# Where the low halves of the expert weights are made: VectorE in place of GpSimd

## The chip, the cores and the metric

The program runs on one core of a Trainium2 chip. The metric is the device time of one execution in microseconds. Five engines work on it, each through its own queue in order: TensorE (PE in the profile, its weight loads PEld), VectorE (DVE), ScalarE (ACT), GpSimd (POOL), and SyncE (SP), which here only issues transfers.

## The reference

A small attention in two resolutions makes a matrix `x` of 4608 tokens by 512; the tokens are then dealt out to 8 experts, 576 to each, and each expert is a two-layer network. The part that matters here, cut to its core:

```python
def _moe_ref(x, w_gate, w1, w2):            # w1: (8, 512, 1024), w2: (8, 1024, 512)
    N, D = x.shape
    E = w_gate.shape[1]
    cap = N // E
    order = np.argsort(-(x @ w_gate).flatten())
    ...                                     # best (token, expert) pairs first, until an expert is full
    for e in range(E):
        mask = assigned == e
        h = np.maximum(x[mask] @ w1[e], 0.0)
        out[mask] = h @ w2[e]
```

## The kernel before, in words

The first part (class `Attention`, up to about 294 us) makes `x`, writes it to memory and keeps the logits of all tokens. The second part has two strands that run into each other.

*Routing* (class `Routing`, lines 626 to 995) finds the tokens of one expert after another, and each list depends on the one before. `setup` prepares keys. `count` narrows a threshold in three steps, twice for each expert: VectorE compares the keys with a row of thresholds (`cmp`, line 702); TensorE counts them (line 728); VectorE brings the counts back (`cs`, line 734); TensorE adds them up (line 737); VectorE compares with the capacity (`fl`, line 740); TensorE spreads the answer (line 742); VectorE takes the maximum (`nj`, line 744) and makes the next thresholds (`thr`, `rest`, lines 748 and 751), the last time the value (`val`, line 755). Then the number of the expert is known (`ei`, line 853), which starts the loads of its weights. `emit` turns the chosen tokens into the list `idx`: VectorE makes one-hot rows (`ohh`, `r`, `ohl`, lines 970 to 982), TensorE multiplies them (line 985), and line 994 writes the list.

*Experts* (class `Experts`). `weights` loads the raw weights into `nat`, four pieces of 128 x 2048 for each expert out of a pool of six. `gather` fetches the tokens' rows with GpSimd's indirect transfers (`xg`, line 1062), makes a high half on ScalarE and a low half on VectorE (`xs`, lines 1081 and 1082), and has SP transpose them (`xt`, line 1083). `mlp` multiplies in fp16 with halves: 192 matmuls `pH` (line 1098) for the hidden layer, with `ht` made by ScalarE and VectorE after each of eight groups (lines 1111 and 1114), then 120 matmuls `pX` (line 1127) for the output `y` (line 1132), which GpSimd scatters to memory (line 1135).

`split` makes the halves of the weights, in eight pieces `k` of 128 x 1024. `wh` is the high half and `wl` the low one, the scaled weight less `wh`. For the first four pieces of the first expert (`FV`) ScalarE writes `wh` straight from the raw weights and VectorE makes `wl` in one instruction. For the 60 others ScalarE first scales the raw weights in place (line 1045), then casts them to `wh` (line 1046), and GpSimd subtracts in four pieces of `LOP` = 256 columns (line 1048).

When `split` runs is set in the loop over the experts: the pieces of expert i + 1 are asked for behind `ht` of group f of expert i (`in1`), or, while the first expert runs, behind the outputs `y` (`in2`). The order on each engine comes from a scheduler with priorities: routing has the higher priority, and other work is put where the scheduler expects an engine to be free. The order is fixed when the program is built.

Of the kernel before, what the change touches and what calls it, by code (L numbers as in the profile page):

```python
# [11 lines left out]
AF = mybir.ActivationFunctionType  # L12
OP = mybir.AluOpType
# [605 lines left out]

W1S, W2S, XM = 64.0, 64.0, 8.0  # L620
LOP = 256
CAP = NTOK // E
LV = ((64, 1024), (32, 32), (32, 1))
SW = 16
HALF = {16: ((0, NT),), 32: ((0, 20), (20, NT)), 64: ((0, 20), (20, NT)), 128: ((0, 12), (12, 24), (24, NT))}
LOV = ()
FV = (0, 1, 2, 3)
XSB = 2
LOE = "vector"
RACT = True  # L630
# [367 lines left out]
class Experts:  # L998
# [32 lines left out]
    def split(self, raw, first):  # L1031

        nc = self.nc
        w = {}

        def piece(k):
            r = raw[k // 2][:, 1024 * (k % 2):1024 * (k % 2) + 1024]
            hi = self.wt.tile([128, 1024], F16, name=f"wh{k}")
            lo = self.wt.tile([128, 1024], F16, name=f"wl{k}")
            sc = W1S if k < 4 else W2S  # L1040
            if first and k in FV or k in LOV:
                nc.scalar.activation(hi, r, AF.Copy, scale=sc)
                nc.vector.scalar_tensor_tensor(lo, r, sc, hi, op0=OP.mult, op1=OP.subtract)
            else:
                nc.scalar.activation(r, r, AF.Copy, scale=sc)  # L1045
                nc.scalar.copy(hi, r)  # L1046
                for a in range(0, 1024, LOP):
                    nc.gpsimd.tensor_tensor(lo[:, a:a + LOP], r[:, a:a + LOP], hi[:, a:a + LOP], op=OP.subtract)  # L1048
            w[k] = (hi, lo)

        return w, piece
# [217 lines left out]
```

## Time and profile before

| what | us |
|---|---|
| three runs | 824.54, 828.63, 828.93 (median 828.63) |
| the profiled execution | 830.1 |
| its span in the trace | 828.3 |
| TensorE busy | 691.8 |
| VectorE busy | 531.8 |
| ScalarE busy | 394.0 |
| GpSimd busy | 401.7 |
| mean granted clock of TensorE | 0.923 |

An engine's busy time is the union of its instructions. A row of a group reads: line, engine, operation, output and inputs by the program's names, shapes, how many; then the busy time and the mean of one in ns; then the idle time of the engine just before them and what ended it. A row of stretches has the stretch in us from the span's start, its length, then busy time and number of instructions for each engine, the granted clock, the share of the transfer engines and GB/s. A row of the timeline has start, duration, engine, line and what it does; in the chain of waits, start, duration, engine and line.

The first matmul of an expert starts at 332.6 us. The first list is written at 322.3 us, the last at 620.4.

### The profile page before, as it was taken

Reading aid. Unit: us, or ns where it says so; the run is one execution under the profiler, and the core shown is the slowest. Engines: PE = TensorE matmul, PEld = TensorE weight load, DVE = VectorE, ACT = ScalarE, POOL = GpSimd, SP = SyncE. Lnnn points to the kernel's source line nnn. Section 1 sums busy time; section 2 is a strip of 40 time slices with the busy share of each in tenths; the row PEclk is TensorE's granted clock in tenths of the full one; section 3 lists DMA queues with packets and bytes.
Section 4 is the critical chain, followed back from the end, with each engine's and each line's share of the span. In section 5 each row is a group of like instructions: output and inputs, shape, how many; then the busy total and the mean of one; then the engine's idle time right before and its main releaser. Section 6 shows DMA issues by size and latency. Waiting matters only on the chain.

```text
span 828.3 us, 21421 instructions
## 1 busy us (share of the span) xinstructions
PE 691.8 (84%) x8545; PEld 473.2 (57%) x8545; DVE 531.8 (64%) x1555; ACT 394.0 (48%) x691; POOL 401.7 (48%) x514
## 2 busy tenths in 40 slices
PE   6688979887898832997888967798989999999995
PEld 4577868776786731653364445445536657474752
DVE  6878888986879878787795758969682222122210
ACT  3356757565485412535564225425625638284210
POOL 8355373562635403417758335436544838474001
PEclk9689999998999965999897999999999999999998
DMA  9949979899897614317352570565184563703101
GB/s 256 204 141 227 275 191 274 214 220 259 193 262 193 188 40 132 130 66 215 90 210 58 124 252 9 196 154 172 53 194 82 205 169 102 160 13 87 29 15 44
DMA packets 152904, 126.19 MB, mean 152 GB/s; under 512 B 96997, under 2 KB 127205, under 8 KB 152805
## 3 DMA queue, kind: packets, MB, share of 16 engines
q1 hardware_dynamic: 145424, 103.30, 48.7%
q0 software_dynamic: 6432, 20.98, 8.2%
q8 instruction: 68, 1.11, 0.6%
q10 hardware_dynamic: 948, 0.55, 0.2%
q14 instruction: 32, 0.25, 0.1%
HBM read 95.30 MB, written 21.23 MB: 141 GB/s over the span
## 4 chain that ended last, share of the span: by engine, by line
PE 37%; DVE 27%; DMA 14%; issue 11%; ACT 4%; SPq 3%; POOL 2%; another core or an unknown queue 1%; ACTq 0%; POOLq 0%; DVEq 0%
PE pH L1098 14%; PE pX L1127 8%; DVE cmp L702 4%; DMA xt<-xs 3%; PE pR L728 2%; DMA nat<-in_v_dram 2%; PE g L476 2%; DVE ht L1114 2%; PE g L436 1%; DMA vw<-in_v_dram 1%; PE g L292 1%; SPq L200 1%; DMA up_dram<-xu 1%; DMA nat<-in_q_dram 1%; PE g L373 1%
## 5 line engine op out<-in xcount | busy, mean ns | idle before, releaser
L1098 PE MATMUL pH<-xt,wh 128*128 128x256 f16 (+1 forms) x1024 | 203.8, 294 | 1.8 <-DMA xt<-xs 0.8
L1048 POOL TENSOR_TENSOR wl<-nat,wh 128x256 f16<-128x256 f32 x240 | 163.1, 712 | 77.1 <-issue 45.1
L1127 PE MATMUL pX<-wh,ht 128*128 128x512 f16 (+1 forms) x640 | 185.6, 386 | 0.0
L1098 PE MATMUL pH<-xt,wl 128*128 128x320 f16 (+1 forms) x512 | 150.0, 293 | 0.0
L1127 PEld LDWEIGHTS <-ht 128*128 128x128 f16 (+1 forms) x960 | 82.1, 101 | 88.2 <-issue 6.7
L1127 PE MATMUL pX<-wl,ht 128*128 128x512 f16 (+1 forms) x320 | 120.0, 386 | 0.0
L1098 PEld LDWEIGHTS <-wh 128*128 128x128 f16 x1024 | 99.8, 100 | 32.5 <-issue 7.0
L1135 POOL DMA_INDIRECT out_dram<-y,idx x40 | 44.9, 1121 | 135.6 <-ACT y L1132 115.7
L1114 DVE SCALAR_TENSOR_TENSOR ht<-pH,ht 128x512 f16<-128x512 f32 (+1 forms) x128 | 52.4, 450 | 70.7 <-ACT ht L1111 70.5
L1111 ACT ACTIVATE ht<-pH 128x512 f16<-128x512 f32 (+1 forms) x128 | 45.5, 407 | 97.1 <-PE pH L1098 97.1
L1132 ACT ACTIVATE y<-pX 128x512 f32<-128x512 f32 (+1 forms) x40 | 23.8, 594 | 132.5 <-PE pX L1127 107.4
L1062 POOL DMA_INDIRECT xg<-x_dram,idx x40 | 42.4, 1059 | 64.4 <-DMA nat<-in_moe_w_dram 32.3
L1046 ACT CAST wh<-nat 128x1024 f16<-128x1024 f32 x60 | 62.5, 1044 | 1.5
L1045 ACT ACTIVATE nat<-nat 128x1024 f32<-128x1024 f32 x60 | 62.8, 1058 | 0.0
L465 ACT COPY pt<-g 64x512 f32<-64x512 f32 x72 | 41.8, 581 | 37.4 <-PE g L454 36.3
L1098 PEld LDWEIGHTS <-wl 128*128 128x128 f16 x512 | 51.1, 100 | 12.8
L1082 DVE SCALAR_TENSOR_TENSOR xs<-xg,xs 128x512 f16<-128x512 f32 (+1 forms) x35 | 23.9, 701 | 53.6 <-ACT xs L1081 46.4
L292 PE MATMUL g<-ident,nat 128*128 128x128 f32 x256 | 41.0, 287 | 15.3 <-DMA nat<-in_q_dram 11.7
L265 POOL TENSOR_TENSOR gtmp<-kt 128x576 f32<-128x576 f32 x7 | 8.3, 1186 | 85.9 <-ACT kt L278 50.6
L476 PE MATMUL g<-vw,pt 128*64 128x65 f32 x1152 | 46.8, 236 | 2.6 <-DMA up_dram<-xu 1.4
L265 POOL TENSOR_TENSOR gtmp<-qz 64x576 f32<-64x576 f32 x28 | 32.4, 1157 | 29.5 <-DVE kdt L268 27.8
L476 PEld LDWEIGHTS g<-vw,pt 128*64 128x64 f32 x1152 | 41.6, 149 | 8.9 <-ACT pt L465 5.1
(222 smaller groups left out, 1282.4 us busy)
## 6 DMA issues: line engine op xcount, KB each, us to landing
nat<-in_moe_w_dram SPq DMA_DIRECT2D x28, 1024.0 KB
vw<-in_v_dram SPq DMA_DIRECT2D x136, 96.0 KB
up<-up_dram SPq DMA_DIRECT2D x36, 256.0 KB
x_dram<-x SPq DMA_DIRECT2D x36, 256.0 KB
nat<-in_q_dram SPq DMA_DIRECT2D x16, 512.0 KB
nat<-in_k_dram SPq DMA_DIRECT2D x16, 512.0 KB
nat<-in_v_dram SPq DMA_DIRECT2D x14, 512.0 KB
up_dram<-xu SPq DMA_DIRECT2D x16, 128.0 KB
```

Source lines behind the costliest of these rows:

```text
L292: nc.tensor.transpose(p[:, a, :, fp], src[:, 4 * hh + 2 * a + s, 2 * fp:2 * fp + 2].rearrange("p f d -> p (f d)"), self.ident)
L465: self.nc.scalar.copy(out, in_)
L476: nc.tensor.matmul(o[64 * i:64 * i + 64, 65 * h:65 * h + 65], pt[:, 2 * g + i, h].rearrange("p b q -> p (b q)"), self.vw[u % 4][:, i, 4 * ...
L1045: nc.scalar.activation(r, r, AF.Copy, scale=sc)
L1046: nc.scalar.copy(hi, r)
L1048: nc.gpsimd.tensor_tensor(lo[:, a:a + LOP], r[:, a:a + LOP], hi[:, a:a + LOP], op=OP.subtract)
L1062: self.fetched = nc.gpsimd.indirect_dma_start(out=xg[:n], out_offset=None, in_=self.x, in_offset=bass.IndirectOffsetOnAxis(ap=idx[:n, c:c ...
L1098: mm = nc.tensor.matmul(p[:, s, :s1 - s0], w[d][a][:, 128 * f:128 * f + 128], xt[:, b, d, s0:s1], start=j == 0, stop=j == len(seq) - 1)
L1111: last = nc.scalar.activation(hi, q, AF.Relu)
L1114: nc.vector.scalar_tensor_tensor(lo, q, 0.0, hi, op0=OP.max, op1=OP.subtract)
L1127: nc.tensor.matmul(p[o:o + m], ht[:, f, h0:h0 + m], w[4 + f // 2][b][:, 512 * (f % 2):512 * (f % 2) + 512], start=j < parts, stop=j >= len ...
L1135: i = nc.gpsimd.indirect_dma_start(out=self.out, in_=y[:n], in_offset=None, out_offset=bass.IndirectOffsetOnAxis(ap=idx[:n, c:c + 1], axis=0))
```

## The change

Every piece of every expert is now made as the first four were: ScalarE writes `wh` from the raw weights in one pass with the scale, and VectorE makes `wl` from the raw weights and `wh`, but in two instructions of 512 columns instead of one of 1024. There is no scaling pass any more, the raw weights are not written, and GpSimd has only its indirect transfers, the loads of the first expert's second layer and what it does in the attention.

```diff
-LOP = 256
+LOP = 512
-LOV = ()
-FV = (0, 1, 2, 3)
...
-            if first and k in FV or k in LOV:
-                nc.scalar.activation(hi, r, AF.Copy, scale=sc)
-                nc.vector.scalar_tensor_tensor(lo, r, sc, hi, op0=OP.mult, op1=OP.subtract)
-            else:
-                nc.scalar.activation(r, r, AF.Copy, scale=sc)
-                nc.scalar.copy(hi, r)
-                for a in range(0, 1024, LOP):
-                    nc.gpsimd.tensor_tensor(lo[:, a:a + LOP], r[:, a:a + LOP], hi[:, a:a + LOP], op=OP.subtract)
+            nc.scalar.activation(hi, r, AF.Copy, scale=sc)
+            for a in range(0, 1024, LOP):
+                nc.vector.scalar_tensor_tensor(lo[:, a:a + LOP], r[:, a:a + LOP], sc, hi[:, a:a + LOP],
+                                               op0=OP.mult, op1=OP.subtract)
```

The scheduler orders the second part anew. In the changed kernel lines from 627 on are two to six lower than in the profile of before (`cs` 734 is 732, `fl` 740 is 738, `wl` 1048 is 1041).

VectorE, just behind the list `idx` of the second expert, where the count for the third begins. Before:

```order
L734 TENSOR_SCALAR cs<-pR 128x16
L994 TENSOR_TENSOR idx<-sm 32x5
L994 TENSOR_TENSOR idx<-sm 32x4 x2
L740 TENSOR_TENSOR fl<-pR,cap 64x8
L744 TENSOR_REDUCE nj<-pR 128x1
L748 SCALAR_TENSOR_TENSOR thr_6802<-nj,tabs 128x32
L751 SCALAR_TENSOR_TENSOR rest<-nj,tabs 128x33
L702 TENSOR_TENSOR cmp_6806<-xh,thr_6802 128x640
L702 TENSOR_TENSOR cmp_6806<-xh,thr_6802 128x512
```

The same steps now:

```order
L732 TENSOR_SCALAR cs<-pR 128x16
L1041 SCALAR_TENSOR_TENSOR wl_6546<-nat,wh_6545 128x512
L738 TENSOR_TENSOR fl<-pR,cap 64x8
L1041 SCALAR_TENSOR_TENSOR wl_6587<-nat,wh_6586 128x512
L742 TENSOR_REDUCE nj<-pR 128x1
L1041 SCALAR_TENSOR_TENSOR wl_6587<-nat,wh_6586 128x512
L746 SCALAR_TENSOR_TENSOR thr_6770<-nj,tabs 128x32
L749 SCALAR_TENSOR_TENSOR rest<-nj,tabs 128x33
L1041 SCALAR_TENSOR_TENSOR wl_6592<-nat,wh_6591 128x512
L700 TENSOR_TENSOR cmp_6774<-xh,thr_6770 128x640
L700 TENSOR_TENSOR cmp_6774<-xh,thr_6770 128x512
```

Four pieces of 512 columns of the low halves of the second expert's weights now stand between the steps of the count that finds the third expert. It goes on so, on VectorE in the changed kernel:

```order
L1076 SCALAR_TENSOR_TENSOR xs<-xg,xs 128x512 x2
L732 TENSOR_SCALAR cs<-pR 128x32
L1041 SCALAR_TENSOR_TENSOR wl_6592<-nat,wh_6591 128x512
L738 TENSOR_TENSOR fl<-pR,cap 32x8
L1041 SCALAR_TENSOR_TENSOR wl_6629<-nat,wh_6628 128x512
L742 TENSOR_REDUCE nj<-pR 128x1
```

In the next step, too, a piece now stands ahead of `fl` and of `nj`, where the kernel before had none.

TensorE at the same place, between the sums of the counts (line 737) and the spreading of the answer (line 742). Before:

```order
L737 MATMUL pR<-cs,id_5478 32x8
L1127 LDWEIGHTS ht
L1127 MATMUL pX<-wh_6277,ht 128x512
L1127 LDWEIGHTS ht
L1127 MATMUL pX<-wh_6277,ht 128x512
L742 LDWEIGHTS one
L742 MATMUL pR<-fl,one 128x8
```

Now:

```order
L735 MATMUL pR<-cs,id_5478 32x8
L1121 LDWEIGHTS ht
L1121 MATMUL pX<-wh_6383,ht 128x512
L1121 LDWEIGHTS ht
L1121 MATMUL pX<-wl_6384,ht 128x512
L1121 LDWEIGHTS ht
L1121 MATMUL pX<-wh_6383,ht 128x512
L740 LDWEIGHTS one
L740 MATMUL pR<-fl,one 128x8
```

TensorE has three matmuls of the experts there instead of two; over the whole routed part it has 960 `pH` and 502 `pX` up to the last list, where it had 768 and 434.

GpSimd, from the second expert's gathers on. Before:

```order
L1062 DMA xg<-x_dram,idx 128x512 x4
L1062 DMA xg<-x_dram,idx 64x512
L1135 DMA out_dram<-y,idx 4608x512
L1048 TENSOR_TENSOR wl_6601<-nat,wh_6600 128x256 x4
L1048 TENSOR_TENSOR wl_6609<-nat,wh_6608 128x256 x4
L1135 DMA out_dram<-y,idx 4608x512
L1048 TENSOR_TENSOR wl_6649<-nat,wh_6648 128x256 x4
L1048 TENSOR_TENSOR wl_6657<-nat,wh_6656 128x256 x4
L1135 DMA out_dram<-y,idx 4608x512
```

Now:

```order
L1056 DMA xg<-x_dram,idx 128x512 x4
L1056 DMA xg<-x_dram,idx 64x512
L1129 DMA out_dram<-y,idx 4608x512 x3
L1056 DMA xg<-x_dram,idx 128x512 x4
L1056 DMA xg<-x_dram,idx 64x512
```

Only gathers and scatters are left in its queue.

## The prediction

> **What bounds the kernel now.** I read the page's engine totals, then its slices of time.
>
> ```profile
> PE 691.8 (84%) x8545; PEld 473.2 (57%) x8545; DVE 531.8 (64%) x1555; ACT 394.0 (48%) x691; POOL 401.7 (48%) x514
> PE   6688979887898832997888967798989999999995
> DVE  6878888986879878787795758969682222122210
> ```
>
> The experts fill the last 24 slices. In the first fourteen of them VectorE stands at 5 to 9 and TensorE at 6 to 9; in the last ten VectorE has almost nothing to do and TensorE is full. The border is the end of routing, so I cut there with the view by stretches: the second, fourth, fifth, sixth and seventh list of tokens (each stretch from one `idx` to the next), the whole routed stretch, and the rest.
>
> ```profile
> core 0: us, PE busy (x) PEld busy (x) DVE busy (x) ACT busy (x) POOL busy (x), PEclk, DMA share, GB/s
> 383.10:436.00 52.90, 43.97 (x321) 24.16 (x320) 42.06 (x121) 29.30 (x44) 35.40 (x45) 0.87 0.51 142
> 483.00:537.00 54.00, 39.78 (x362) 25.91 (x358) 40.24 (x124) 23.34 (x37) 28.74 (x38) 0.94 0.38 137
> 537.00:576.30 39.30, 34.86 (x289) 18.65 (x289) 31.46 (x115) 14.74 (x26) 19.24 (x18) 1.00 0.55 146
> 576.30:611.90 35.60, 32.44 (x288) 18.81 (x285) 27.87 (x111) 16.43 (x25) 19.25 (x27) 1.00 0.37 118
> 611.90:620.50 8.60, 6.60 (x41) 3.14 (x40) 5.97 (x19) 1.76 (x3) 3.47 (x3) 0.89 1.20 210
> 332.60:620.50 287.90, 243.36 (x1961) 138.96 (x1961) 222.55 (x743) 123.76 (x200) 150.15 (x187) 0.94 0.47 137
> 620.50:818.40 197.90, 196.87 (x1295) 120.91 (x1293) 39.94 (x85) 92.26 (x151) 93.53 (x129) 1.00 0.36 94
> ```
>
> After 620.5 TensorE idles 1.0 us: that part only loses if something becomes late. Before it, TensorE idles 287.9 - 243.4 = 44.5 us; the second and fourth lists cost 8.9 and 14.2 of it, the fifth and sixth 4.4 and 3.2. The same stretches for the experts' own matmuls (line 1098, then line 1127), and the chain of waits for two full halves of an expert:
>
> ```profile
> 332.60:620.50 287.90, 118.33 (x768) 71.45 (x767) 0.94 0.47 137
> 332.60:620.50 287.90, 103.98 (x434) 35.91 (x435) 0.94 0.47 137
> 628.95 23.62 PE pH L1098 x192
> 652.58 23.43 PE pX L1127 x120
> ```
>
> At 0.123 and 0.195 us each they need 768 x 0.123 + 434 x 0.195 = 179.2 us of the 287.9. Routing and transposes take 243.4 - 179.2 = 64.2, idling 44.5. Who waits there, from the view of waits (engine line, releaser, us in total, times, longest):
>
> ```profile
> POOL wl L1048 <- ACT wh L1046: 23.3, 6, 9.7
> PEld L728 <- DVE cmp L702: 17.5, 24, 2.3
> DVE nj L744 <- PE pR L742: 16.2, 33, 0.9
> DVE fl L740 <- PE pR L737: 12.1, 25, 1.3
> PE pR L728 <- DVE cmp L702: 9.3, 14, 2.0
> DVE cs L734 <- PE pR L728: 8.6, 20, 1.6
> PE pR L985 <- DVE ohl L982: 7.6, 5, 5.3
> ```
>
> TensorE waits for VectorE's comparisons and one-hot rows (`cmp`, `ohl`); VectorE waits back in short gaps of about half a microsecond (`nj`, `fl`, `cs`, 36.9 us). So the bound there is a chain going back and forth between the two, with TensorE's matmuls in a fixed order around it.
>
> **Why VectorE is slow there.** Two pairs of rows of VectorE's timeline, and GpSimd's beside the second:
>
> ```profile
> 360.39 0.83 DVE L702 TENSOR_TENSOR cmp<-xl,thr 128x640 bf16<-128x640 int16 x2
> 405.90 3.38 DVE L702 TENSOR_TENSOR cmp<-xl,thr 128x640 bf16<-128x640 int16 x2
> 363.37 0.16 DVE L755 TENSOR_TENSOR val<-nj,rest 128x1 f32<-128x1 f32 x1
> 394.77 1.33 DVE L755 TENSOR_TENSOR val<-nj,rest 128x1 f32<-128x1 f32 x1
> 319.18 0.75 DVE L982 TENSOR_TENSOR ohl<-pl,io 128x576 bf16<-128x576 int16 x1
> 406.44 2.55 POOL L1048 TENSOR_TENSOR wl<-nat,wh 128x256 f16<-128x256 f32 x4
> ```
>
> The same pair of instructions takes 0.83 us alone and 3.38 while GpSimd subtracts; one element costs 1.33 instead of 0.16. Groups by shape from 332 to 620 us:
>
> ```profile
> L982 DVE TENSOR_TENSOR ohl<-pl,io 128x576 bf16<-128x576 int16 x14 | 13.2, 952 | 0.0
> L702 DVE TENSOR_TENSOR cmp<-xl,thr 128x512 bf16<-128x512 int16 x12 | 8.0, 669 | 0.0
> L755 DVE TENSOR_TENSOR val<-nj,rest 128x1 f32<-128x1 f32 x12 | 3.9, 325 | 0.4
> ```
>
> Taking off their calm durations (0.75, 0.42 and 0.16 us) leaves 2.8 + 3.0 + 2.0 = 7.8 us; the same subtraction over all the shapes of that view gives about 37 us. So VectorE's 222.6 us hold between 7.8 and 37 of collision with GpSimd; I take 37, since the excess sits almost wholly in instructions that overlap a subtraction. With 7.8 alone VectorE's need below would be 277 us instead of 248, 3 us short of TensorE's. [...]
>
> **The change part by part.**
>
> ```profile
> L1048 POOL TENSOR_TENSOR wl<-nat,wh 128x256 f16<-128x256 f32 x240 | 163.1, 712 | 77.1 <-issue 45.1 <-ACT wh L1046 23.3 <-POOL wl L1048 8.5
> L1045 ACT ACTIVATE nat<-nat 128x1024 f32<-128x1024 f32 x60 | 62.8, 1058 | 0.0
> L1062 POOL DMA_INDIRECT xg<-x_dram,idx x40 | 42.4, 1059 | 64.4 <-DMA nat<-in_moe_w_dram 32.3 <-DVE xs L1082 18.4 <-issue 5.5
> L1082 DVE SCALAR_TENSOR_TENSOR xs<-xg,xs 128x512 f16<-128x512 f32 (+1 forms) x35 | 23.9, 701 | 53.6 <-ACT xs L1081 46.4 <-DMA xg<-x_dram,idx 6.4 <-issue 0.7
> 326.24 1.22 DVE L1043 SCALAR_TENSOR_TENSOR wl<-nat,wh 128x1024 f16<-128x1024 f32 x1
> ```
>
> Removed: 240 subtractions on GpSimd (163.1 us), and 60 scalings on ScalarE (62.8 us). GpSimd's own time is free; what counts is the collision. ScalarE is 43% busy in the routed stretch (123.8 of 287.9), so its saving is hidden, except that a low half can begin 1.06 us earlier. GpSimd keeps its gathers and scatters of about 1.1 us, no longer queued behind subtractions; that is hidden by the matmuls between `idx` and the next expert.
>
> Added: 128 pieces of 512 columns less the four whole ones. Price of one: no row shows it, but `xs` is the same operation on the same types and size, 0.70 us; half of the whole piece (1.22) is 0.61. Between neighbours the ends overlap, so I take 0.62. The first eight stand ahead of 332 us, 0.16 us more per whole piece, covered by the wait for the gathered rows. By the order of the new program 88 of the 128 stand in the routed part, 32 after it beside full matmuls (20 us on an engine that has 158 us free).
>
> Moved: the routed part now ends later in the experts' work. By the order TensorE has 960 `pH` and 502 `pX` matmuls of the experts up to the last list, not 768 and 434: 118.1 + 98.0 = 216.1 us, with 576 and 458 left (160.3). So TensorE needs 216.1 + 64.2 = 280.3 us in it. VectorE needs 222.6 - 37 + 88 x 0.62 + 8 (eight more pairs of `ht` at about 0.8, three `xs`) = 248. In the order a piece now stands ahead of nearly every `fl`, `nj` and `thr` of the second list, that is in the 0.5 us gaps; each delays the chain by some 0.2 us, while TensorE got more matmuls there.
>
> What TensorE then idles: at least 0; at most what VectorE's whole old idling (287.9 - 222.6 = 65.3) would cause, 248 + 65.3 - 280.3 = 33. I take the rate of the calmest list, 3.2 us for each of six plus 2.0 for the last (short) one, 21.2, since GpSimd no longer collides. Gain 44.5 - 21.2 = 23.3.
>
> New waits: `wl` now waits in VectorE's queue for `wh` of ScalarE and the weights' loads, with routing behind it. How far ahead the loads are, from the timelines of VectorE and SP (the expert's number, the loads, the one-hot rows):
>
> ```profile
> 366.76 0.14 DVE L853 TENSOR_SCALAR ei<-code 1x1 int32<-1x1 f32 x1
> 367.70 2.43 SPq L1025 DMA_DIRECT2D nat<-in_moe_w_dram  x4
> 377.36 2.36 DVE L982 TENSOR_TENSOR ohl<-pl,io 128x576 bf16<-128x576 int16 x2
> ```
>
> The loads are issued 1 to 3.4 us after the number; by the order the first `wl` stands behind the `ohl` rows, 13 us after it. So I cost this 0 and price the other case below. On SP the first two loads of the last expert now stand ahead of the transposes for the sixth; they wait for `wl` pieces that end before those transposes are ready: 0. At the border of the first two experts ScalarE's last `xs` now stands behind the last `y`, and VectorE, SP and TensorE's first `pH` over the later columns wait for it: 0 to 4 us, I take 1.5.
>
> Clock: TensorE's granted clock is 0.94 in the routed stretch and 1.00 after it, 0.87 where it idles much: about 0.06 x 288 = 17 us at most. With half the idling I take 4, between 0 and 17. [...] TensorE's longest wait in the list of 0.87:
>
> ```profile
> PE pR L728 <- DVE cmp L702: 3.3, 3, 2.0
> ```
>
> [...]
>
> **Sum** against the profiled execution (830.1 us, of which the span is 828.3): 828.3 - 23.3 + 1.5 - 4 = 802.5, 25.8 less. The median of the three runs is 828.6, so the forecast is 803 us.
>
> **Rivals.** 1. VectorE full: its short gaps are not filled but added to, all 65.3 us of idling stay. TensorE then idles 33 us: 828.6 - 11.5 + 1.5 = 819 us. For it: 248 of 280 us is 88% busy; against it: pieces stand in the very gaps.
> 2. Slower: GpSimd's waits for `wh` (23.3 us, one of 9.7) come over to VectorE's queue, with `fl`, `nj` and `cmp` behind them, on top of rival 1. TensorE idles 33 + 23.3 = 56.3: 828.6 + 11.8 + 1.5 = 842 us. It decides from VectorE idling some 75 us in the routed part. For it: a queue in order; against it: those waits came from ScalarE standing behind matmuls, and GpSimd was ahead of its time.
> 3. Nothing: the collision is off the path and the chain is bound by round trips; then the new pieces cost what the collision did, 828 us. Against it: in us, idling goes with GpSimd's work (8.9 and 14.2 beside 35.4 and 28.7, but 4.4 and 3.2 beside 19.2 and 19.3). For it: as a share of its stretch GpSimd is as busy in the sixth list (54%) as in the fourth (53%).
>
> **Numbers.** Forecast (788 to 814) 0.61, rival 1 0.16, rival 2 0.14, rival 3 0.09. Within 0.5% is 4 us, about what a measurement can tell here. Faster takes the forecast and rival 1, 0.77; same 0.09; slower 0.14. The range leaves out rival 2 and a little below: low 787 is an idling of 10 us and 8 us of clock (828.6 - 34.5 - 8 + 1.5), high 829.
>
> **What would show it.** No subtraction on GpSimd; `cmp` of 512 columns at 0.42 us throughout, `val` at 0.16; `wl` at 0.6 to 0.7 us; the last `idx` near 632, not 620 (332.6 + 280.3 + 21.2 + 1.5 - 4), but 160 us of full matmuls behind it, not 198; TensorE idling about 21 us ahead of it; the clock above 0.94. The forecast is wrong if VectorE's waits for `wh` or for SP's loads reach 20 us, or TensorE's waits for `fl` and `cs` grow to what `cmp` lost.

## The result, and the profile after

The changed kernel takes 802.43 us in the median of four runs (797.46 to 807.51). Beside it the kernel before took 828.78. The ratio is 0.968, interval 0.9624 to 0.9737. The profiled execution is one of the two short ones: 797.6 us with a span of 795.8.

The totals of the engines and their slices of time, from the page after:

```profile
PE 682.5 (86%) x8545; PEld 470.8 (59%) x8545; DVE 561.6 (71%) x1679; ACT 333.2 (42%) x631; POOL 236.9 (30%) x274
PE   6687979797898853599789799999899979999994
DVE  6878887887788877788769689888869235172210
```

GpSimd loses 165 us, ScalarE 61, VectorE gains 30. The stretches that answer to those of before follow, in the same columns: the second, fourth, fifth, sixth and seventh list, the whole routed part, and what stands behind it.

```profile
382.10:434.80 52.70, 45.42 (x385) 28.07 (x382) 41.66 (x143) 22.33 (x40) 9.19 (x8) 0.94 0.50 150
484.90:526.20 41.30, 40.70 (x327) 21.97 (x323) 37.31 (x131) 12.76 (x24) 11.25 (x10) 1.00 0.55 157
526.20:572.80 46.60, 44.08 (x385) 26.92 (x385) 40.95 (x145) 18.76 (x35) 8.24 (x7) 1.00 0.45 140
572.80:611.20 38.40, 37.94 (x347) 24.26 (x344) 30.23 (x123) 13.40 (x24) 7.98 (x8) 1.00 0.68 197
611.20:621.40 10.20, 9.87 (x62) 4.83 (x60) 9.97 (x27) 3.29 (x6) 1.77 (x2) 1.00 0.53 151
330.70:621.40 290.70, 272.40 (x2238) 161.44 (x2238) 242.76 (x851) 105.14 (x194) 54.37 (x49) 0.97 0.51 153
621.40:786.00 164.60, 158.11 (x1018) 95.51 (x1016) 51.35 (x97) 50.34 (x96) 26.53 (x28) 0.99 0.35 83
```

The routed part is as long as before (290.7 us against 287.9), but TensorE does more in it: of the experts' own matmuls 960 `pH` and 520 `pX`, against 768 and 434. It idles 18.3 us instead of 44.5. What is left behind it is 164.6 us and not 197.9. There a new idle time of some 6 us has come in, where 1.0 was. The fourth list, which had lost 14.2 us of TensorE's time, loses 0.6 now.

VectorE's short instructions from 332 to 620 us by shape, and the pieces of the low halves in the whole program:

```profile
L980 DVE TENSOR_TENSOR ohl<-pl,io 128x576 bf16<-128x576 int16 x14 | 10.2, 750 | 0.0
L700 DVE TENSOR_TENSOR cmp<-xl,thr 128x512 bf16<-128x512 int16 x12 | 5.0, 417 | 0.0
L753 DVE TENSOR_TENSOR val<-nj,rest 128x1 f32<-128x1 f32 x12 | 1.9, 155 | 0.2
L1041 DVE SCALAR_TENSOR_TENSOR wl<-nat,wh 128x512 f16<-128x512 f32 x128 | 85.2, 683 | 2.6 <-ACT wh L1039 0.2
```

All three are at their calm durations, 0.75, 0.42 and 0.16 us, where their means had been 0.95, 0.67 and 0.33. The last row also answers rival 2: ahead of 128 pieces VectorE waited 2.6 us in all. The view of waits for the routed part:

```profile
DVE nj L742 <- PE pR L740: 11.7, 21, 0.9
ACT xs L1075 <- DMA xt<-xs: 10.7, 8, 2.5
DVE cs L732 <- PE pR L726: 6.7, 13, 1.6
DVE fl L738 <- PE pR L735: 6.6, 15, 0.6
PEld L726 <- DVE cmp L700: 5.9, 15, 1.2
```

TensorE's weight loads had waited 17.5 us for `cmp`; now it is 5.9. VectorE's own gaps ahead of `nj`, `fl` and `cs` shrank from 36.9 to 25.0 us, since pieces stand in them. The second row is a wait that has grown, from 4.5 us before: ScalarE's `xs` waits until a transpose has read the old rows and the buffer is free.

The new idle time behind the last list, in the view of TensorE's waits from 621.4 us on; then the timelines of SP and of ScalarE:

```profile
PE pH L1092 <- DMA xt<-xs: 4.9, 2, 4.7
```

```profile
612.98 6.81 SPq L1023 DMA_DIRECT2D nat<-in_moe_w_dram  x2
620.38 20.95 SPq L1077 DMA_TRANSPOSE xt<-xs  x5
```

```profile
618.95 1.14 ACT L1075 ACTIVATE xs<-xg 128x512 f16<-128x512 f32 x2
632.91 0.63 ACT L1075 ACTIVATE xs<-xg 128x512 f16<-128x512 f32 x1 [8.67 <-DMA xg<-x_dram,idx]
638.76 0.63 ACT L1075 ACTIVATE xs<-xg 64x512 f16<-64x512 f32 x1 [3.69 <-DMA xt<-xs]
```

Two loads of 1 MB for the last expert are issued just ahead of the transposes for the sixth. From the first to the last issue the five transposes then take 21 us, and TensorE stands 4.7 us at 639 us. For the wait of 8.67 us the view names a gather, but the sixth expert's own gathers were issued from 573.1 to 578.2 us. What the third `xs` needs is one of the two `xs` buffers, and so the end of the first transpose, some 12 us after its issue; this is read from the order and the buffers, no row says it. Transfers on GpSimd's queue were late as well: the gather issued at 622.06 us landed 10.8 us later, where the 25 gathers from 340 to 600 us took 4.1 in the middle and 9.3 at most.

### The profile page after: what moved, and what is told of

Read it like the earlier page. It is cut to its first block, busy times and chain, and to the rows that moved or that the text cites. A ratio compares the mean times of both kernels' runs of the same rounds, so it can differ in the third digit from the quotient of the medians.

```text
span 795.8 us, 21153 instructions
## 1 busy us (share of the span) xinstructions
PE 682.5 (86%) x8545; PEld 470.8 (59%) x8545; DVE 561.6 (71%) x1679; ACT 333.2 (42%) x631; POOL 236.9 (30%) x274
## 4 chain that ended last, share of the span: by engine, by line
issue 30%; PE 29%; DVE 17%; DMA 12%; ACT 5%; POOL 5%; SPq 1%; POOLq 0%; ACTq 0%; DVEq 0%
PE pH L1092 6%; PE pX L1121 4%; DMA xt<-xs 3%; POOL out_dram L1129 3%; PE g L292 2%; PE g L476 2%; PE g L436 2%; PE g L325 2%; DVE cmp L700 2%; PE g L454 1%; PE pR L726 1%; PE g L373 1%; DMA xg<-x_dram,idx 1%; DMA nat<-in_q_dram 1%; PE g L494 1%
## 5 line engine op out<-in xcount | busy, mean ns | idle before, releaser
L1092 PE MATMUL pH<-xt,wh 128*128 128x256 f16 (+1 forms) x1024 | 200.3, 291 | 7.1 <-DMA xt<-xs 6.4
L1121 PE MATMUL pX<-wh,ht 128*128 128x512 f16 (+1 forms) x640 | 183.0, 382 | 1.2 <-ACT y L1126 1.2
L1092 PEld LDWEIGHTS <-wh 128*128 128x128 f16 x1024 | 98.1, 99 | 35.0 <-issue 10.8
L1041 DVE SCALAR_TENSOR_TENSOR wl<-nat,wh 128x512 f16<-128x512 f32 x128 | 85.2, 683 | 2.6 <-ACT wh L1039 0.2
L1039 ACT ACTIVATE wh<-nat 128x1024 f16<-128x1024 f32 x64 | 66.8, 1056 | 5.8 <-DMA nat<-in_moe_w_dram 5.7
L476 PE MATMUL g<-vw,pt 128*64 128x65 f32 x1152 | 44.4, 229 | 4.2 <-issue 1.9
L476 PEld LDWEIGHTS g<-vw,pt 128*64 128x64 f32 x1152 | 39.3, 142 | 10.2 <-ACT pt L465 4.7
L278 ACT COPY kt<-g 64x512 f32<-64x512 f32 (+1 forms) x56 | 35.1, 626 | 19.3 <-PE g L292 12.7
L278 ACT COPY qz<-g 64x512 f32<-64x512 f32 (+1 forms) x52 | 33.0, 634 | 19.6 <-PE g L292 19.0
```

The source lines that it names most:

```text
L278: self.nc.scalar.copy(out, in_)
L476: nc.tensor.matmul(o[64 * i:64 * i + 64, 65 * h:65 * h + 65], pt[:, 2 * g + i, h].rearrange("p b q -> p (b q)"), self.vw[u % 4][:, i, 4 * ...
L1041: nc.vector.scalar_tensor_tensor(lo[:, a:a + LOP], r[:, a:a + LOP], sc, hi[:, a:a + LOP], op0=OP.mult, op1=OP.subtract)
L1092: mm = nc.tensor.matmul(p[:, s, :s1 - s0], w[d][a][:, 128 * f:128 * f + 128], xt[:, b, d, s0:s1], start=j == 0, stop=j == len(seq) - 1)
L1121: nc.tensor.matmul(p[o:o + m], ht[:, f, h0:h0 + m], w[4 + f // 2][b][:, 512 * (f % 2):512 * (f % 2) + 512], start=j < parts, stop=j >= len ...
```

## The experiments

The theory (A): GpSimd's subtractions hold VectorE's short instructions up, those sit on the chain between VectorE and TensorE, and the pieces cost little in their place. Rivals: (B) the gain is something else than the collision; (C) it is ScalarE's scaling pass that is gone; (D) the pieces on VectorE are themselves dear. The runs with idle work on GpSimd and the one that moves loads keep the order of the other engines, by the traces. The others change what the scheduler sees, and VectorE's order in their traces is another one over long stretches: a few us of difference in these can come from the order alone.

**The changed kernel again.**

> The changed kernel once more, to see how its own runs scatter and to have a second trace. Every theory: 797 to 808 us. If the scatter is one place and not noise all over, a slower trace should differ from the first mainly there; I expect it behind the end of routing, where TensorE waited for the transposed rows of the sixth expert.

803.25 us (800.07 to 804.57), ratio 0.9674 [0.9611, 0.9738]. TensorE idles 20.1 us in the routed part and 7.0 behind it, so both readings stand in a second profile. The first `pH` starts at 333.6 us against 330.7: 2.9 of the 4.4 us between the two spans lie ahead of the experts, and not behind the end of routing, as expected.

**GpSimd's subtractions back, without use.**

```diff
+            if not (first and k < 4):
+                for a in range(0, 1024, 256):
+                    nc.gpsimd.tensor_tensor(self.dlo, self.dr, hi[:, a:a + 256], op=OP.subtract)
```

> The changed kernel, with the 240 subtractions of 256 columns put back on GpSimd as idle work: they read the high halves and a constant tile, and write a tile that nobody reads. The order on TensorE, VectorE, ScalarE and SP is unchanged. Theory A (the gain is the end of the collisions between GpSimd and VectorE): VectorE's cmp, thr, val stretch again, by 30 us or more together, TensorE idles 40 to 55 us in the routed part instead of 18, time 826 to 845. Rival B (the gain is the new order of the engines, GpSimd does not matter): 798 to 808, as without the idle work.

859.2 us, ratio 1.0367 [1.0291, 1.0444]: 57 us more than without, beyond what A had expected. The routed part, then `cmp` by shortest, middle and longest duration in ns, then two groups:

```profile
329.70:680.70 351.00, 288.20 (x2233) 164.68 (x2233) 302.69 (x851) 105.07 (x194) 205.47 (x225) 0.92 0.41 127
```

```profile
L700 DVE TENSOR_TENSOR cmp<-xh,thr x28: 407/688/1009, 299.6 to 627.1; 128x640 bf16<-128x640 int16 x14, 128x512 bf16<-128x512 int16 x14
```

```profile
L1048 POOL TENSOR_TENSOR dlo<-dr,wh 128x256 f16<-128x256 f32 x240 | 209.7, 874 | 76.9 <-ACT wh L1042 59.7
L1044 DVE SCALAR_TENSOR_TENSOR wl<-nat,wh 128x512 f16<-128x512 f32 x128 | 111.3, 887 | 2.1
```

The same 851 instructions of VectorE take 302.7 us instead of 242.8, and TensorE idles 62.8 instead of 18.3. The pieces collide too: 887 ns in the mean, not 683. With the order of the other engines unchanged, the gain is gone: B, as far as it puts the gain down to that order, is refuted. Not all of the 57 us is the collision, though:

```profile
ACT xs L1081 <- DMA xg<-x_dram,idx: 19.6, 4, 9.3
```

The gathers stand in GpSimd's queue behind the subtractions, which wait for `wh`, and `xs` waits 19.6 us for them, where it waited 3.5. How the 57 us divide between the two is not shown; the waits for gathers grew by 16. In the kernel before, the same row of the routed part is small, so there late gathers are no rival to the collision:

```profile
ACT xs L1081 <- DMA xg<-x_dram,idx: 2.2, 2, 1.4
```

**The same with memsets.** 240 memsets of 128 x 768 on GpSimd in the same places of the code; they only write. (The idle subtractions were of 128 x 256; the text below names another size for them.)

```diff
+                for a in range(0, 1024, 256):
+                    nc.gpsimd.memset(self.dm, 0.0)
```

> The changed kernel with 240 idle GpSimd memsets of 128x768 float32, in the places where the second run had idle subtractions of 128x768: GpSimd is as much in use, but its work only writes SBUF and reads none; the orders on TensorE, VectorE, ScalarE and SP are those of the changed kernel. If it is GpSimd's reading subtractions that stretch VectorE's instructions: the first cmp of each list stays near 0.45 us, the wl near 0.68, and the time is 800 to 815 (gathers may start a little later behind the memsets). If any long work of GpSimd on SBUF does it: cmp and wl stretch as in the run with the subtractions (884 at the middle, up to 1.5 us), and the time is 830 or more. Only this second outcome would make 'no work for GpSimd' a rule for every kind of its work.

809.18 us, ratio 0.9758 [0.9658, 0.9859]. GpSimd is busy as long in the routed part as with the subtractions (207 us and 205); the memsets do not wait for `wh`, and GpSimd idles 15.4 us ahead of them by their row, where it idled 76.9 ahead of the subtractions. The kernel is 6 to 7 us longer than without, with intervals that overlap.

```profile
334.00:631.60 297.60, 272.19 (x2239) 160.79 (x2239) 252.80 (x851) 105.29 (x194) 207.20 (x255) 0.98 0.49 149
```

```profile
L700 DVE TENSOR_TENSOR cmp<-xh,thr x28: 408/448/493, 303.1 to 589.3; 128x640 bf16<-128x640 int16 x14, 128x512 bf16<-128x512 int16 x14
L823 DVE CAST kh<-h x7: 183/755/761, 298.9 to 572.0; 128x36 int16<-128x36 int32 x6, 128x10 int16<-128x10 int32 x1
L738 DVE TENSOR_TENSOR fl<-pR,cap x21: 145/153/158, 302.3 to 590.9; 32x8 bf16<-32x8 f32 x14, 64x8 bf16<-64x8 f32 x7
```

This `cmp`, with two inputs in SBUF, is not touched (448 ns in the middle, 446 without the memsets, 688 with the subtractions); `kh`, a cast with one input, goes from 170 to 755 ns; `fl`, which reads PSUM, is as ever, and so it was beside the subtractions (144 to 158 ns). So a busy GpSimd alone did not make this kernel slow (809.18 us), and the subtractions did (859.2). The memsets read nothing, but they differ from the subtractions in operation and size as well, so which of these counts is not shown. Over the whole program `xs` waits 15.3 us for gathers here, 12.2 without the memsets and 25.0 with the subtractions.

The memsets do stretch others. Take, shape by shape in the routed part, what VectorE's instructions last longer in the mean than in the changed kernel, times their number: 30 us with the memsets (casts and one-input instructions of 36 columns above all), 61 with the subtractions (18 of it the pieces), and 37 in the kernel before. The 30 us cost the kernel 6 to 7, so the sum of the stretching does not give the price; that it depends on where the instructions stand in the chain is argued, not shown.

**No low halves at all.** The pieces on VectorE are left out, and a constant tile stands for `wl`.

```diff
-            lo = self.wt.tile([128, 1024], F16, name=f"wl{k}")
+            lo = self.lz
-            for a in range(0, 1024, LOP):
-                nc.vector.scalar_tensor_tensor(...)
```

> The changed kernel without the low halves of the weights: VectorE makes none, the matmuls read one constant tile instead (that part of the product is left out). Theory A: VectorE's pieces cost the chain some 0.1 to 0.2 us each of 88, of which most is covered by matmuls: 790 to 798. Rival D (VectorE is full in the routed part, 243 of 291 us, and its pieces set the time): 55 us less work shows, 770 to 785. If they are wholly hidden: 800 to 806.

783.34 us, ratio 0.9438 [0.9382, 0.9495]. So without the subtractions and without anything in their place some 46 us would go, and the pieces take about 20 of them back. That misses A's 790 to 798 and lies inside D's 770 to 785. Still, VectorE does 60 us less in the routed part and 20 show: neither theory has it quite, and the order is another one, too.

```profile
329.20:568.90 239.70, 226.82 (x1943) 131.64 (x1943) 182.34 (x730) 85.99 (x160) 51.21 (x43) 0.98 0.54 164
568.90:766.60 197.70, 197.70 (x1304) 121.66 (x1302) 39.86 (x84) 67.67 (x126) 32.12 (x34) 1.00 0.35 93
```

With the experts' matmuls taken off (768 and 426, at 0.123 and 0.195 us) the routed part has 62.0 us of other things and of idling, against 71.2 in the changed kernel. Behind the last list nothing idles here, where the changed kernel idles 6 us.

**ScalarE's scaling pass kept.** ScalarE scales and then casts as before, VectorE subtracts in 512 columns.

```diff
...
+                nc.scalar.activation(r, r, AF.Copy, scale=sc)
+                nc.scalar.copy(hi, r)
+                for a in range(0, 1024, LOP):
+                    nc.vector.tensor_tensor(lo[:, a:a + LOP], r[:, a:a + LOP], hi[:, a:a + LOP], op=OP.subtract)
```

> The changed kernel with ScalarE's scaling pass put back (scale in place, cast, and VectorE subtracts in pieces of 512), so that only the engine of the subtraction differs from the kernel before. Theory A: ScalarE's second pass is hidden, 800 to 808. Rival C (part of the gain is the shorter path over ScalarE to the high half and to ht): 812 to 820, half of the gain back.

796.76 us, ratio 0.9616 [0.9553, 0.9679]: no slower, and even below A's 800 to 808. ScalarE has its 60 us again (393.1 us busy in all), and TensorE idles 15.7 us in the routed part. C, which had 812 to 820, is refuted; the pass was hidden, as costed.

**The size of the pieces.** `LOP` 1024 and 256 instead of 512.

> The changed kernel with VectorE's low halves whole, 1024 columns in one instruction instead of two of 512. 44 instructions fewer in the routed part, each some 0.1 us of fixed cost less, but one piece now stands 1.2 us ahead of a routing step instead of 0.7. Theory A (what counts is how the pieces fit into the gaps of 0.5 us): even or a little slower, 802 to 812. Rival D (VectorE's total work counts): 796 to 800.

> The same with pieces of 256 columns: 176 in the routed part, some 0.4 us each, about 10 us more of VectorE's time in all. Theory A: 800 to 806. Rival D: 808 to 815.

1024: 798.88 us, 0.9597 [0.9556, 0.9638]. 256: 804.01 us, 0.965 [0.9602, 0.9697]. The first lies in D's range, the second in A's; around 0.968 [0.9624, 0.9737] for 512 columns neither can be told apart safely, so the sizes do not decide between A and D. Two pieces of 512 columns take 2 x 0.683 us by their row, where one of 1024 took 1.22 in the kernel before, 0.15 less. TensorE idles 21.0 and 25.4 us in the routed part, 0.8 and 0.1 behind it: what one place gains the other loses.

**Four buffers for `xs`.**

```diff
-XSB = 2
+XSB = 4
```

> The changed kernel with four buffers for xs instead of two, so that ScalarE need not wait for a transpose to land before it writes the next xs. If TensorE's 6 us of waiting for the transposed rows of the sixth expert come from that wait: 795 to 799, with under 2 us of idling behind the last list. If the transposes themselves are slow behind the loads: 800 to 805, the idling stays.

787.51 us, ratio 0.9462 [0.9415, 0.951], more gain than expected. Its profiled execution took 799.04 us, longer than its other four (785.07 to 789.34), so the profile below is from a repeat.

> The kernel with four xs buffers again, for a second profile. 785 to 790 us as in the fast ones of its first runs; TensorE idle in the routed part 8 to 14 us against 18.3 with two buffers, and the wait behind the last list still there (4 to 8 us).

783.97 us (782.58 to 784.41), ratio 0.9413 [0.9335, 0.9491]. Its two parts:

```profile
335.20:616.10 280.90, 268.83 (x2239) 160.25 (x2239) 242.20 (x851) 104.53 (x194) 56.83 (x50) 0.99 0.53 162
616.10:772.30 156.20, 156.16 (x1017) 94.75 (x1015) 51.01 (x96) 49.59 (x95) 26.38 (x27) 1.00 0.32 79
```

VectorE has the same 242 us of work, but TensorE idles 12.1 us instead of 18.3 and has a clock of 0.99; behind the last list it idles nothing, where a wait of 4 to 8 us had been expected. Its time lies below that of both kernels.

**The last expert's loads behind the transposes.** Only SP's order differs.

```diff
-                        idx2, raw = ro.phase(i + 2 == E, False, lambda ei: ex.weights(ei, False))
+                        def known(ei):
+                            with tc.issue_after(ex.tl[24].ins) if i + 2 == E else nullcontext():
+                                return ex.weights(ei, False)
+                        idx2, raw = ro.phase(i + 2 == E, False, known)
```

> The changed kernel with the last expert's weight loads put behind the transposes of the sixth expert on SP; the order on every other engine is the same. If the loads that are issued just ahead of these transposes hold them up: 795 to 799. If they do not, as the prediction said: 801 to 805.

797.41 us (796.44 to 800.05), ratio 0.9592 [0.9546, 0.9638]. SP now:

```profile
627.42 13.51 SPq L1078 DMA_TRANSPOSE xt<-xs  x5
642.03 1.02 SPq L1024 DMA_DIRECT2D nat<-in_moe_w_dram  x2
```

The transposes take 13.5 us from the first to the last issue and not 21, and TensorE idles 0.0 us behind the last list. So the loads did hold the transposes up. Whether that comes from their place in SP's queue or from the load on the transfer engines is open: the late gather at 622.06 us of the changed kernel came through another queue. In this profile TensorE idles 25.8 us in the routed part, though, against 18.3 and 20.1, with one wait of 5.2 us for `fl`; the intervals of the two ratios overlap, and how much the kernel gains from it is open.

**Both together, and with 1024 columns.** The two edits above, and those with `LOP = 1024`.

> Four xs buffers and the last expert's loads behind the sixth expert's transposes, together. If the two remove different waits (xs buffers those inside the routed part, the loads' place those behind the last list): the 787.5 of four buffers alone less the 5 to 6 us that TensorE waits behind the last list, 778 to 786. If the waits are one and the same: 786 to 790, as with four buffers alone.

> As the run before, with pieces of 1024 columns instead of 512. If the longer pieces' waits ahead of the gates' small VectorE instructions count (about 0.6 us more on each of some thirty waits in the routed part): 5 to 15 us longer than the run before. If what counts is VectorE's total time (32 fixed costs of some 0.06 us fewer in the routed part): 0 to 3 us shorter. With 512 columns and two buffers the two sizes differed by less than 5 us either way.

Both: 782.11 us, 0.9384 [0.9305, 0.9464]. That is in the range for two different waits, but no different from the repeat of four buffers alone (783.97 us): these had already removed the wait behind the last list. With 1024 columns 799.56 us, 0.9618 [0.9536, 0.97], some 17 us more, outside both ranges. The profiles show 7.8 of it (spans of 794.8 and 787.0), 6.1 of that behind the last list; the rest has no trace. TensorE's waits there, and SP:

```profile
PE pH L1094 <- DMA xt<-xs: 6.1, 1, 6.1
```

```profile
615.90 4.65 SPq L1078 DMA_TRANSPOSE xt<-xs  x2
620.75 0.44 SPq L1024 DMA_DIRECT2D nat<-in_moe_w_dram  x1
622.83 4.79 SPq L1078 DMA_TRANSPOSE xt<-xs  x2
627.81 0.62 SPq L1024 DMA_DIRECT2D nat<-in_moe_w_dram  x1
628.67 2.71 SPq L1078 DMA_TRANSPOSE xt<-xs  x1
```

The scheduler has put four loads, which the run before issued from 600.63 us on, just ahead of the transposes and between them, and the same wait is back, in spite of four buffers. So this run changes SP's order too, and does not tell what the longer pieces cost by themselves.

## Why the prediction was right, and where its errors cancelled

The forecast was 803 us and the median is 802.43. The terms of its sum, against the profile of after:

| term | predicted, us | measured, us |
|---|---|---|
| up to the first `pH` | 0 | -1.9 (332.6 to 330.7; +1.0 in the second profile) |
| TensorE idle in the routed part, the border of the first two experts in it | -23.3 + 1.5 | -26.2 (44.5 to 18.3; -24.4 in the second) |
| TensorE busy there with other than the experts' matmuls (clock) | -4 | -11.3 (64.2 to 52.9) |
| behind the last list | 0 | +7.1 (length less the experts' matmuls: 0.9 before, 8.0 after) |
| together | -25.8 | -32.3 |

The span fell by 32.5 us, 6.7 more than the forecast of 25.8 (by the second profile it fell by 28.1). By the medians the fall is 26.4 us, since the profiled execution after lies 4.8 us below its median and that of before 1.3 above its own. So the direction and the main step are right, but that the number came out within 1 us is luck: the clock's term and SP's were each wrong by some 7 us in opposite directions, and the rest lies within the scatter of the runs.

- **The collision.** The step that carries the forecast was right: idle time of 21.2 us predicted, 18.3 and 20.1 measured. That all 37 us of collision would go with the subtractions was the author's estimate; they did: shape by shape, VectorE's instructions of the kernel before last 37 us longer in sum than the same ones now. VectorE in the routed part was to be 248 us and is 242.8, although the pieces are dearer, since more of its instructions overlap at their ends (its durations add up to 37 us more than its busy time before, and to 50 now). The lower bound of 7.8 us is excluded by the same sum.
- **The pieces.** 0.62 us each predicted, 0.683 by the row. That they fill gaps holds only in part: against leaving them out they cost about 20 of their 60 us, the wait behind the last list among it.
- **The clock, mis-sized.** The term was 4 us, with 17 as the most. The stretches' rows give the loss, as an estimate: 0.06 x 288 = 17 us before, 0.03 x 291 = 9 after, so some 8 less. TensorE's busy time beside the experts' matmuls fell by 11.3; where the other 3 come from is not shown. If the loss went with the idling, which no row shows, half of the 17 would have been 8.5; the sum took 4, with no row behind that choice. The stretch of the second list still has a clock of 0.94, and TensorE's longest wait in it, by the view of waits, is this one:

```profile
PE pR L726 <- DVE ol L890: 1.8, 1, 1.8
```

  In the same stretch of the kernel before it was 2.0 us, at a clock of 0.87. What lowers the clock in these stretches is not shown.
- **SP, costed at 0 and wrong.** The reason given was that the pieces which the two loads wait for end before the transposes are ready. So it was: the loads were issued 7.4 and 1.0 us ahead of the first transpose. But the step counted their issue and not their transfer: the transposes were spread over 21 us and TensorE lost some 6 us. Moving the loads (13.5 us, and 0.0 us of idling behind the last list) shows it, and loads between the transposes in the last run bring it back.
- **The border of the first two experts.** 1.5 us taken; `pH` waits 1.15 us for `xt` at 394 us. Right.
- **Waits for `wh` and for loads, costed at 0.** 2.6 us ahead of all pieces: right, and rival 2 (842 us) never came near its condition, some 75 us of VectorE idling in the routed part: it idles 47.9.
- **The last `idx` near 632.** It was written at 621.4, although 18 more `pX` (3.5 us) than foreseen stand ahead of it. Of these 14 us the clock's term is 7.3, the idling 4.4 and the earlier first `pH` 1.9.
- **Rival 3** is refuted by the idle subtractions (ScalarE's waits for gathers grew by 16 of their 57 us only), rival 1 by the 18.3 us of idling where it had 33.

## What to carry to other kernels

Price a second engine's work by what it does to the instructions beside it. Here 163 us of subtractions, on an engine that had time to spare, cost some 46 us, as leaving them out shows; the traces put it down to short instructions on a chain between two engines, which they stretched. Memsets on the same engine (178 us) cost some 7. When work moves onto the engine of that chain, look for what then comes up next: here buffers for `xs`, whose waits rose from 4.5 to 10.7 us in the routed part, and two more of which, with the order that the scheduler then made, were worth some 15 to 20 us. And count a load as done when its transfer has landed, not when it is issued: two loads issued just ahead of transposes were no "0", as the transposes took 21 us behind them and 13.5 ahead of them.

## What the runs showed of the hardware that was not expected

- What GpSimd did decided which VectorE instructions it stretched: subtractions took the `cmp` that reads `xh` to 0.69 us in the middle, memsets left it at 0.45 and took the cast `kh` to 0.755. Whether subtractions stretch `kh` is not seen, as none ran beside one. But they stretched more than instructions with two tensors: in the kernel before, `e` (line 890, one tensor of 128 x 36 and one value per partition) took 0.61 us in the four of seven that ran beside a subtraction, and 0.23 to 0.24 in the other three. `fl`, which reads PSUM, stayed at 0.15 us beside both. Two others that read PSUM did not: with the memsets `ad` (line 939, 128 x 36) took 0.40 us in the mean and `v` (line 960, 128 x 36) 0.33, where the changed kernel has 0.25 and 0.18; with the subtractions they stayed at 0.25 and 0.18.
- The stretching seems to go both ways: 240 subtractions of 128 x 256 took 712 ns in the mean before, and 874 in the run where VectorE had the pieces (there they read a constant tile in place of the raw weights).
- TensorE's granted clock fell to 0.94 in a stretch in which it never waited longer than 1.8 us for another engine.
- Four runs of one program fell at 797.5, 797.6, 807.2 and 807.5 us. Its second series lay between 800.1 and 804.6. What sets this was not found; the two profiles differ mostly ahead of the experts.
